# Windowed attention and a GEGLU block on one core: eight-token rows for the dilated heads, masks made on GpSimd, sums in banks of their own

## The chip, the core and the metric

The kernel runs on one core of a Trainium2 chip. A core has five engines with instruction streams of their own: TensorE (PE in the profile: matrix multiplies, with PEld for its weight loads), VectorE (DVE), ScalarE (ACT), GpSimd (POOL) and SyncE (SP, which here only issues DMAs). On-chip memory is SBUF, with 128 partitions; TensorE writes its results to PSUM, which has 8 banks of 512 fp32 columns per partition. DMA queues, fed by SP, ACT and POOL, bring data from HBM.

The metric is the time of one execution on the device, in microseconds. Three executions of the kernel before took 361.88, 362.62 and 362.64 us; the median is 362.62.

## What is computed

Attention with a causal window over 8 batches, 8 heads, 576 tokens and head size 64, then a gated FFN over the 4608 tokens. Heads 0 to 3 are plain: a query sees the last 32 keys. Heads 4 to 7 are dilated: it sees every fourth of the last 128 keys.

```python
scores = scale * np.matmul(q, k.transpose(0, 1, 3, 2))
rel = pos[:, None] - pos[None, :]
mask_plain = (rel >= 0) & (rel < window)                                       # window 32
mask_dil = (rel >= 0) & (rel < window * dilation) & (rel % dilation == 0)      # dilation 4
...
attn = attn / (np.sum(attn, axis=-1, keepdims=True) + 1e-09)
x = (attn @ v) reordered to (4608 tokens, 512)
...
gelu = 0.5 * g * (1.0 + erf(g * inv_sqrt2))      # g = x @ w_gate, d_ff = 1536
val = x @ w_val
return (gelu * val @ w_out)
```

Inputs and outputs are fp32; matmuls run on fp16 operands.

## The kernel before

**Unit of attention.** The work is cut into 32 pairs of heads, four to a batch: pair n belongs to batch n // 4, and its first two pairs are plain, the other two dilated. For a pair, `emit_s` writes scores (keys on partitions, queries on columns) into four PSUM banks and ACT takes the Exp into an fp16 tile `P`. Masking is done in one of two ways: TensorE first adds a bias (`bias_p` or `bias_d`, made from the masks) through the identity matrix, or DVE multiplies `P` by `mask_p` or `mask_d` (L379). `emit_pv` multiplies `P` with v (numerators, "num") and with a matrix of ones (the sums, "den"); both have 64 output partitions per head, so the two heads of a pair stand one above the other. With `wide` the sums have whole banks to themselves. `norm_r` transposes the sums (`dt`), takes reciprocals (`rc`) and spreads them (`rb`); `norm_x` multiplies numerators by `rb` into `xT`, the FFN's input with features on partitions.

**Dilated layout.** Token t belongs to class t mod 4, and a dilated head is a plain window of 32 within a class of 144 tokens. q and k of dilated heads are loaded with four tokens per row (`quads`): 128 rows of four tokens and a rest of 16 rows. `t_dil` transposes the 128 rows, `t_rest` the 16 rows. `kTr` holds the last keys of each class again (`last_keys`).

**The first two batches.** From batch 2 on, q and k are transposed by the DMA (`load_batch_rest`). For batches 0 and 1 TensorE does it with matmuls against the identity: plain heads from rows of six tokens (`sixes`, `t_plain`), dilated heads with `t_dil` and `t_rest`. Batch 0 stands ahead of everything. Its loads go out on SP and ACT: q and k of the plain heads, then of the dilated ones, then v. POOL issues loads of the identities and of the two masks, which the kernel carries as constants, then makes `bias_d`, casts the dilated q, issues the rest of v and the weights of block 0, casts v, and issues the other weights. DVE makes `bias_p`. TensorE runs 16 dummy matmuls (`warm`, L583) meanwhile. Then the four pairs of batch 0 follow in an order written out by hand, quoted below, in which the sums of pairs 0, 1, 2 and 3 go one after the other to the same banks (6 and 7), between other work.

```python
emit_s(0, 4, pe_mask=True); emit_s(1, 0, pe_mask=True)
...
den(0, 4, wide=True)
...                      # t_dil and t_rest of both dilated pairs, last_keys
den(1, 4, wide=True)
emit_s(2, 0, pe_mask=True)
num(0, 4)
den(2, 4, wide=True)
emit_s(3, 0, pe_mask=True)
num(1, 4)
den(3, 4, wide=True)
num(2, 0); num(3, 2)
```

**FFN stages.** The tokens come in 9 chunks (stages) of 512. A stage runs `ffn1` for 12 blocks (8 matmuls each: gate and value, L533; the first two blocks of stages 0 and 1 are interleaved in `ffn1_two`, L545), with Gelu on ACT (L557) and the GEGLU product on DVE (L558, `geglu`), then `ffn2` for four groups of 128 tokens (L564), and stores. Attention of later batches is woven in: `scores` and `values_b` name the pairs that stand in the `ffn2` part, `values_a` those between `ffn1` blocks of stages 3 to 6. Batch 1's transposes stand between the blocks 8 to 11 of stage 0.

**Plain pairs between ffn1 blocks.** Seven plain pairs of `values_a` go through `emit_both` (L455): v of a pair of heads is stored as v, ones, v (`vset`, three sets, the ones written once by DVE at L610 and L611), so that one matmul of full width gives numerators of a head on 64 partitions and its sums on the other 64. `norm_both_r` (L470) and `norm_both_x` (L480) then work on 64 partitions at a time, two instructions for a pair. `values_a` sets these pairs three or four blocks apart.

All instructions run in program order on each engine, across engines by semaphores; every tile of PSUM is one of the 8 banks, addressed by hand, so who waits for whom follows from the bank numbers.

Of the kernel before, what the change touches and what calls it, by code (L numbers as in the profile page):

```python
# [15 lines left out]
WIN = 32  # L16
DIL = 4
USCALE = 32.0


def _np_masks():
    p = np.arange(128)[:, None]

    def band(n, off=0):
        rel = np.arange(n)[None, :] + off - p
        return (rel >= 0) & (rel < WIN)

    main_p, last_p, tail_p = band(160), band(128), band(64, 64)
    main_d = band(128)

    rel = 48 + np.arange(16)[None, :] - p % 64
    rest_d = [(rel >= 0) & (rel < WIN) & (p // 64 == m) for m in range(2)]
    mp = np.concatenate([main_p, main_p, main_p, last_p, tail_p], axis=1).astype(np.float16)
    md = np.concatenate([main_d, rest_d[0], main_d, rest_d[1]], axis=1).astype(np.float16)
    return mp, md
# [3 lines left out]
def kernel(  # L39
# [19 lines left out]
    R6 = S // 6  # L59
    NCH = NT // CH  # L60
# [11 lines left out]
    mp_np, md_np = _np_masks()  # L72
    mp_dram = nc.inline_tensor(mp_np, name="mask_plain")
    md_dram = nc.inline_tensor(md_np, name="mask_dil")
    id_dram = nc.inline_tensor(np.eye(P, dtype=np.float16), name="attn_identity")
    id32_dram = nc.inline_tensor(np.eye(16, dtype=np.float32), name="identity_f32")

    const = ctx.enter_context(tc.tile_pool(name="const", bufs=1))
    psum = ctx.enter_context(tc.tile_pool(name="psum", bufs=1, space=bass.MemoryType.PSUM))
    ldp = ctx.enter_context(tc.tile_pool(name="ldp", bufs=1))  # L80
    qtp = ctx.enter_context(tc.tile_pool(name="qtp", bufs=2))
# [8 lines left out]
    ident32 = const.tile([16, 16], F32, tag="ident32")  # L90
# [9 lines left out]

    HP = HK // 2
    vset = [
        (
            const.tile([P, 4, HP, 3, D], F16, tag=f"vp{i}", name=f"vp{i}"),
            const.tile([P, HK, 4, D], F16, tag=f"vd{i}", name=f"vd{i}"),
            const.tile([P, HP, 3, D], F16, tag=f"vt{i}", name=f"vt{i}"),
            const.tile([P, HK, 2, D], F16, tag=f"vr{i}", name=f"vr{i}"),
        )
        for i in range(3)
    ]  # L110
# [11 lines left out]
    first_d = [x32[t][:, 0 : HK * 4 * D] for t in range(2)]  # L122
    first_r = [x32[2 + t][0:16, 0 : HK * 4 * D] for t in range(2)]
# [34 lines left out]

    def rows(src, b, kb):
        n = min(P, S - kb * P)  # L160
        return n, src[b, 0:HK, kb * P : kb * P + n, :].rearrange("h p d -> p h d")
# [8 lines left out]
    def new_v(b):  # L170

        sv = ldp.tile([P, 5, HK, D], F32, tag="sv", name=f"sv{b}")
        tiles["v", b] = vset[b % 3]
        return sv
# [6 lines left out]
    def v_cast(b, sv):  # L181
        vp, vd, vt, vr = tiles["v", b]
        nc.gpsimd.tensor_copy(
            vp.rearrange("p j g x d -> p (j g) x d")[:, :, 0:3:2, :],
            sv[:, 0:4].rearrange("p j (g x) d -> p (j g) x d", x=2),
        )
        nc.gpsimd.tensor_copy(vt[:, :, 0:3:2, :], sv[:, 4].rearrange("p (g x) d -> p g x d", x=2))
# [96 lines left out]
    def t_dil(b, hp, qd, q0, k0, engs):  # L284

        qtd_ = tiles["qT", b][1]
        for t, c0 in ((0, q0), (1, k0)):
            for hl in range(2):
                for m in range(2):
                    nc.tensor.transpose(  # L290
                        ps16f[:, c0 + (2 * hl + m) * P : c0 + (2 * hl + m + 1) * P],
                        qd[:, t, 2 * hp + hl, 2 * m : 2 * m + 2, :].rearrange("p r d -> p (r d)"),
                        ident,
                    )
        for t, c0 in ((0, q0), (1, k0)):
            copy(
                engs[t],
                qtd_[:, t, 2 * hp : 2 * hp + 2].rearrange("p h m i -> p (h m) i")[:, :, 0:P],
                ps16f[:, c0 : c0 + 512].rearrange("p (c i) -> p c i", i=P),
            )  # L300

    def t_rest(b, hp, rd, r0):

        qtd_ = tiles["qT", b][1]
        f32 = rd[0].dtype == F32
        pv = (psf if f32 else ps16f)[:, r0 : r0 + P]
        for t in range(2):
            for hl in range(2):
                for m in range(2):
                    c0 = (4 * t + 2 * hl + m) * 16  # L310
                    h0 = (2 * hp + hl) * 4 * D + 2 * m * D
                    nc.tensor.transpose(
                        pv[:, c0 : c0 + 16], rd[t][:, h0 : h0 + P], ident32 if f32 else ident[0:16, 0:16]
                    )
        nc.vector.tensor_copy(
            qtd_[:, :, 2 * hp : 2 * hp + 2].rearrange("p t h m i -> p t (h m) i")[:, :, :, P:NCL],
            pv.rearrange("p (t c i) -> p t c i", t=2, i=16),
        )
# [64 lines left out]
    def emit_pv(n, b0, parts=("num", "den"), wide=False):  # L383
# [17 lines left out]
        if is_plain(n):  # L401
            if "num" in parts:
                for j in range(5):
                    for hl in range(2):
                        lhs = vp[:, j, hp, 2 * hl, :] if j < 4 else vt[:, hp, 2 * hl, :]
# [38 lines left out]
    def emit_both(n, b0):  # L444


        b, hp = n // NHP, n % 2
        pt = tiles["P", n]
        vp, _, vt, _ = tiles["v", b]
        for hl in range(2):  # L450
            for j in range(5):
                w = (PW, PW, PW, P, PT)[j]
                p0 = j * PW - (32 if j == 4 else 0)
                trio = vp[:, j, hp] if j < 4 else vt[:, hp]
                nc.tensor.matmul(  # L455
                    ps[:, b0 + 2 * hl + j // 4, j % 4 * P : j % 4 * P + w],
                    trio[:, hl : hl + 2, :].rearrange("p x d -> p (x d)"),
                    pt[:, hl, p0 : p0 + w],
                    start=j in (0, 4),
                    stop=True,  # L460
                    skip_group_check=True,
                )

    def both_rows(half, b0, hl):
        return psf[64 * half : 64 * half + 64, (b0 + 2 * hl) * 512 : (b0 + 2 * hl) * 512 + S]

    def norm_both_r(n, b0):
        dt = nrm.tile([P, 18, 32], F32, tag="dt", bufs=1)
        for hl in range(2):
            nc.vector.transpose(  # L470
                dt[64 * hl : 64 * hl + 64].rearrange("p b c -> p (b c)"), both_rows(1 - hl, b0, hl)
            )
        recip(n, dt)

    def norm_both_x(n, b0):
        b, hp = divmod(n, NHP)
        rb = tiles.pop(("rb", n))
        for hl in range(2):
            half = slice(64 * hl, 64 * hl + 64)
            nc.vector.tensor_tensor(  # L480
                xT[hp][half, b * S : (b + 1) * S], both_rows(hl, b0, hl), rb[half], ALU.mult
            )

# [9 lines left out]
    def norm_r(n, b0, wide=False):  # L493
# [7 lines left out]
        recip(n, dt)  # L501

    def recip(n, dt):
# [84 lines left out]
    nc.gpsimd.dma_start(ident, id_dram.ap())  # L588
    nc.gpsimd.dma_start(mask_p, mp_dram.ap())
# [10 lines left out]
    qd0 = ldp.tile([P, 2, HK, 4, D], F16, tag="qd", name="qd0")  # L600
    new_qt(0)

    def r4(t):
        return fh(t).rearrange("p h (r d) -> p h r d", r=4)
# [231 lines left out]
```

The softmax here doesn't subtract the row's maximum and nothing guards it: scores larger than these inputs give would overflow.

## Time and profile before

| | |
|---|---|
| profiled execution, device time | 361.88 us |
| its span, first to last instruction | 359.8 us |
| mean granted TensorE clock | 0.985 |
| median of three executions | 362.62 us |
| FFN matmuls, L533 and L564, busy | 100.6 + 100.6 + 100.9 us |
| DVE busy, of it GEGLU products | 196.0 us, 72.6 us |
| POOL busy | 78.2 us |
| HBM read, written | 40.13 MB, 9.44 MB |

The profile is of one execution. A matmul of 512 columns is listed with about 380 ns, but they overlap: 96 of them take 20.72 us in the chain, 216 ns each. So a busy share of TensorE near 100% says that it has no gaps, not that it is at its peak. "Idle before" of an engine that isn't the bottleneck costs nothing. In a timeline, a line gives start, length, engine, line of the code, operation, output and inputs, and in brackets what ended the idle time before it.

### The profile page before, as it was taken

The page shows a single profiled execution, that of the slowest core. Times are in us where ns is not written, and L with a number is a line of the kernel's source. Part 1 is how long each engine was busy: PE and PEld are TensorE (multiplying, and loading weights), DVE is VectorE, ACT ScalarE, POOL GpSimd, SP SyncE. Part 2 cuts the span into 40 slices and gives each one's busy share as a digit, 9 for nine tenths or more (in the row PEclk, how much of TensorE's full clock was granted, in tenths as well). Part 3 has the DMA queues.
Part 4 walks back from the last instruction along what each step waited for, and adds up shares of the span by engine and source line. Part 5 has one row for each costly group of instructions (what it writes and reads, how often), then busy time and mean ns, then how long its engine had stood idle before and what let it go on. Part 6 is the DMA issues. An engine that isn't in the chain of part 4 may idle for free.

```text
span 359.8 us, 5997 instructions
## 1 busy us (share of the span) xinstructions
PE 344.5 (96%) x2358; PEld 166.2 (46%) x2358; DVE 196.0 (54%) x298; ACT 145.9 (41%) x212; POOL 78.2 (22%) x110
## 2 busy tenths in 40 slices
PE   6789999999989999899999999999999999999995
PEld 2554454444544445444444444544454444444442
DVE  3584446744266325765479838893679613403320
ACT  2633355244542345433653356436543123312321
POOL 2580434450531342063003410140000000000000
PEclk9959999999999999999999999999999999999999
DMA  8999999999999897599438952795100020011002
GB/s 208 232 183 215 209 159 195 199 141 239 192 119 228 178 157 144 139 168 153 94 106 186 148 97 88 178 168 68 60 29 0 21 97 2 1 66 52 0 29 87
DMA packets 107291, 45.30 MB, mean 126 GB/s; under 512 B 83040, under 2 KB 102496, under 8 KB 107264
## 3 DMA queue, kind: packets, MB, share of 16 engines
q1 hardware_dynamic: 84272, 31.21, 40.1%
q0 software_dynamic: 21456, 12.01, 25.8%
q10 hardware_dynamic: 1536, 1.70, 2.1%
q8 instruction: 18, 0.29, 0.3%
q14 instruction: 9, 0.07, 0.1%
HBM read 40.13 MB, written 9.44 MB: 138 GB/s over the span
## 4 chain that ended last, share of the span: by engine, by line
PE 88%; DVE 5%; DMA 3%; ACT 1%; issue 1%; ACTq 0%
PE ps L533 47%; PE ps L564 26%; PE ps L442 5%; PE ps L545 4%; DMA xT<-in_k_dram 3%; PE ps L369 2%; PE ps L339 1%; DVE dt L500 1%; DVE rb L507 1%; DVE xT L521 1%; PE ps L355 1%; PE ps L455 1%; PE ps L332 1%; ACT P L371 1%; DVE rc L505 0%
## 5 line engine op out<-in xcount | busy, mean ns | idle before, releaser
L558 DVE SCALAR_TENSOR_TENSOR u_all<-g,ps 128x512 f16<-128x512 f16 x108 | 72.6, 683 | 75.8 <-PE ps L533 65.7
L557 ACT ACTIVATE g<-ps 128x512 f16<-128x512 f32 x108 | 63.6, 597 | 123.6 <-PE ps L533 109.4
L564 PE MATMUL ps<-wo,u_all 128*128 128x512 f16 x432 | 100.9, 380 | 0.4 <-ACT osb L575 0.3
L533 PE MATMUL ps<-xT,wg 128*128 128x512 f16 x392 | 100.6, 379 | 0.2
L533 PE MATMUL ps<-xT,wv 128*128 128x512 f16 x392 | 100.6, 379 | 0.0
L564 PEld LDWEIGHTS <-u_all 128*128 128x128 f16 x432 | 39.2, 98 | 44.6 <-issue 0.5
L533 PEld LDWEIGHTS <-wv 128*128 128x128 f16 x392 | 38.3, 98 | 46.4 <-issue 0.2
L533 PEld LDWEIGHTS <-wg 128*128 128x128 f16 x392 | 37.3, 98 | 44.6 <-issue 2.1
L575 ACT ACTIVATE osb<-ps 128x512 f32<-128x512 f32 x33 | 19.7, 597 | 48.4 <-PE ps L564 48.4
L500 DVE STREAM_TRANSPOSE dt<-ps 128x576 f32<-128x576 f32 x25 | 19.5, 779 | 25.7 <-PE ps L442 25.6
L199 POOL CAST qp<-st 128x2048 f16<-128x2048 f32 x6 | 11.4, 1893 | 99.5 <-DMA st<-in_k_dram 61.3
L507 DVE STREAM_TRANSPOSE rb<-rc 128x576 f32<-128x576 f32 x32 | 24.9, 778 | 1.1
L371 ACT ACTIVATE P<-ps 128x1152 f16<-128x1152 f32 x16 | 18.1, 1129 | 13.1 <-PE ps L369 13.0
L349 ACT ACTIVATE P<-ps 128x960 f16<-128x960 f32 x16 | 15.5, 970 | 9.2 <-PE ps L339 9.1
L521 DVE TENSOR_TENSOR xT<-ps,rb 128x576 f16<-128x576 f32 x16 | 17.8, 1124 | 0.3
L545 PE MATMUL ps<-xT,wg 128*128 128x512 f16 x40 | 16.0, 400 | 1.4 <-DVE xT L521 0.9
L577 DVE TENSOR_SCALAR osb<-ps 128x512 f32<-128x512 f32 x3 | 2.1, 692 | 27.8 <-PE ps L564 27.8
L545 PE MATMUL ps<-xT,wv 128*128 128x512 f16 x40 | 15.9, 398 | 0.0
L442 PE MATMUL ps<-P,ones 128*64 128x192 f16 (+5 forms) x174 | 11.6, 248 | 2.0 <-ACT P L371 1.0
L379 DVE TENSOR_TENSOR P<-P,mask_p 128x1344 f16<-128x1344 f16 x10 | 9.1, 917 | 6.8 <-ACT P L350 6.8
L379 DVE TENSOR_TENSOR P<-P,mask_d 128x1152 f16<-128x1152 f16 x8 | 6.1, 757 | 11.1 <-ACT P L371 11.1
L470 DVE STREAM_TRANSPOSE dt<-ps 64x576 f32<-64x576 f32 x14 | 10.9, 781 | 0.4
(83 smaller groups left out, 268.4 us busy)
## 6 DMA issues: line engine op xcount, KB each, us to landing
out_dram<-osb SPq DMA_DIRECT2D x36, 256.0 KB, 2.0
sv<-in_v_dram SPq DMA_DIRECT2D x40, 128.0 KB, 3.5
st<-in_q_dram SPq DMA_DIRECT2D x24, 128.0 KB, 3.2
st<-in_k_dram SPq DMA_DIRECT2D x24, 128.0 KB, 2.9
qd<-in_q_dram POOLq DMA_DIRECT2D x7, 256.0 KB, 5.0
qd<-in_k_dram POOLq DMA_DIRECT2D x7, 256.0 KB, 6.7
vd<-in_v_dram POOLq DMA_DIRECT2D x7, 256.0 KB, 7.1
wg<-in_moe_w_gate_dram POOLq DMA_DIRECT2D x3, 512.0 KB, 7.7
```

Of the source, the lines that this page charges most:

```text
L349: nc.scalar.activation(pt[:, :, 0:PB], sb[:, 0, :, 0:PB], AF.Exp, bias=0.0, scale=scale)
L371: nc.scalar.activation(pt, ps[:, b0 : b0 + 4, 0:DW], AF.Exp, bias=0.0, scale=scale)
L442: nc.tensor.matmul(o, lhs, rhs, start=st, stop=True, skip_group_check=True)
L500: nc.vector.transpose(dst, den)
L507: nc.vector.transpose(rb.rearrange("p (b c) -> p b c", c=32), bass.AP(tensor=rc.tensor, offset=rc.offset, ap=[rc.ap[0], [1, 18], [0, 32]]),)
L521: nc.vector.tensor_tensor(dst.rearrange("p (i m s) -> p i m s", m=2, s=2), num, rb.rearrange("p (s m i) -> p i m s", s=2, m=2), ALU.mult,)
L533: nc.tensor.matmul(ps[:, b0 + gi, :], w[:, kc, ns], xT[kc][:, tok], start=(kc == 0), stop=(kc == NKC - 1))
L545: nc.tensor.matmul(ps[:, pairs[nb] + gi, :], w[:, kc, ns], xT[kc][:, tok], start=(kc == 0), stop=(kc == NKC - 1),)
L557: nc.scalar.activation(g, ps[:, b0, :], AF.Gelu)
L558: nc.vector.scalar_tensor_tensor(u_all[:, nb, :], g, USCALE, ps[:, b0 + 1, :], ALU.mult, ALU.mult)
L564: nc.tensor.matmul(ps[:, bank, :], u_all[:, fc, tb * P : (tb + 1) * P], wo_t[fc // 4][:, fc % 4, :], start=(fc == 0), stop=(fc == NNB - 1),)
L575: nc.scalar.activation(osb, ps[:, bank, :], AF.Copy, bias=0.0, scale=1.0 / USCALE)
```

## The change

- **Rows of eight tokens.** q and k of the dilated heads of batches 0 and 1 are loaded as 72 rows of eight tokens (`eights`), without a rest. `t_dil` makes 16 transposes of 72 columns for each pair (for q and k together) and two copies of 576 columns; `t_rest` and the fp32 identity are gone. For batch 0 the loads come in two halves of two heads; each half of q and k is cast by one instruction on 72 partitions (`cast_d`): two on DVE, one on POOL, one on ACT, the latter ahead of the first Exp.
- **Masks and identity** are made by POOL with memset and `affine_select`, in place of four loads; `bias_p` moves from DVE to POOL.
- **Batch 0 in another order.** Both dilated pairs are transposed right after the scores of the plain pairs, into banks 4 to 7. The sums of pair 0 go to banks 2 and 3, those of pair 1 to banks 0 and 1, those of pairs 2 and 3 to banks 6 and 7. The numerators of pairs 0 and 1 leave PSUM by an ACT copy, and POOL multiplies them (`num_split`). The weights of block 1 are issued ahead of POOL's casts of v, and those of block 2 after batch 0.
- **Plain pairs between ffn1 blocks** use `emit_pv(..., wide=True)`, `norm_r` and `norm_x` like the dilated ones: 10 matmuls for numerators and 6 for sums, of half width. The ones within v are gone, and v's tiles come from a pool of three. `values_a` sets pairs of stages 5 and 6 two blocks apart.
- `warm` has 20 matmuls instead of 16.

```diff
-    nc.gpsimd.dma_start(ident, id_dram.ap())
-    nc.gpsimd.dma_start(mask_p, mp_dram.ap())
...
+    nc.gpsimd.memset(ident, 1.0)
+    for sign in (1, -1):
+        nc.gpsimd.affine_select(
+            out=ident, in_=ident, pattern=[[sign, P]], compare_op=ALU.is_ge, fill=0.0, base=0, channel_multiplier=-sign
+        )
+    def band(t, step, off):
+        for sign, base in ((1, off), (-1, WIN - 1 - off)):
+            nc.gpsimd.affine_select(
...
+    nc.gpsimd.memset(mask_p, 1.0)
+    band(mask_p[:, 0:PB].rearrange("p (r c) -> p r c", c=PW), 0, 0)
+    band(mask_p[:, PB : PB + P].rearrange("p (r c) -> p r c", r=1), 0, 0)
+    band(mask_p[:, PB + P : PH].rearrange("p (r c) -> p r c", r=1), 0, 64)
+    nc.gpsimd.tensor_scalar(bias_p, mask_p, 1.0, 60000.0, ALU.subtract, ALU.mult)
+    nc.gpsimd.memset(mask_d, 1.0)
+    by_class = mask_d.rearrange("p (m i) -> p m i", m=2)
+    band(by_class[:, :, 0:P], 0, 0)
+    band(by_class[:, :, P:NCL], 64, 48)
+    nc.gpsimd.tensor_scalar(bias_d, mask_d, 1.0, 60000.0, ALU.subtract, ALU.mult)
...
+    def eights(src, b, h0, h1):
+        return src[b, h0:h1, :, :].rearrange("h (p r) d -> p h (r d)", r=8)
...
+        for t in range(2):
             for hl in range(2):
-                for m in range(2):
+                for r in range(4):
+                    c0 = ((hl * 2 + r % 2) * 2 + r // 2) * R8
                     nc.tensor.transpose(
...
+                        ps16[:, b0 + t, c0 : c0 + R8],
+                        q8[:, t, 2 * hp + hl, 2 * r : 2 * r + 2, :].rearrange("p r d -> p (r d)"),
+                        ident[0:R8, 0:R8],
...
-    warm(16, 7)
+    warm(20, 7)
...
+    cast_d("pool", 0, 0)
+    cast_d("dve", 1, 0)
+    cast_d("act", 1, 1)
+    cast_d("dve", 0, 1)
     load_v_dil_rest(0)
     load_w(0)
-    v_cast(0, sv0)
-    copy("pool", tiles["v", 0][1], r4(first_vd))
     w1 = load_w(1)
-    load_w(2)
...
+    def num_split(n, b0):
+        emit_pv(n, b0, ("num",))
+        rb = tiles.pop(("rb", n))
+        nc.scalar.copy(first_n[n], psf[:, b0 * 512 : b0 * 512 + S])
+        nc.gpsimd.tensor_tensor(xT[n][:, 0:S], first_n[n], rb, ALU.mult)
...
     emit_s(0, 4, pe_mask=True)
     emit_s(1, 0, pe_mask=True)
...
+    t_dil(0, 0, qd0, 4, ("dve", "dve"))
+    t_dil(0, 1, qd0, 6, ("act", "act"))
+    last_keys(0, 0, 2)
+    last_keys(0, 2, HK, nc.gpsimd)
+    v_cast(0, sv0)
+    copy("pool", tiles["v", 0][1], r4(first_vd))
+
+    den(0, 0, wide=True)
+    den(1, -2, wide=True)
+    emit_s(2, 4, pe_mask=True)
+    emit_s(3, 0, pe_mask=True)
+    den(2, 4, wide=True)
+    num_split(0, 4)
+    num_split(1, 4)
     den(3, 4, wide=True)
     num(2, 0)
     num(3, 2)
+    load_w(2)
...
-    values_a = {3: {4: 16}, 4: {2: 20, 6: 21}, 5: {1: 24, 4: 25, 7: 26}, 6: {1: 28, 4: 29, 7: 30, 10: 31}}
+    values_a = {3: {4: 16}, 4: {3: 20, 6: 21}, 5: {2: 24, 4: 25, 6: 26}, 6: {1: 28, 3: 29, 5: 30, 7: 31}}
...
-                (norm_both_x if is_plain(pend) else norm_x)(pend, SB)
+                norm_x(pend, SB)
...
-                if is_plain(pend):
-                    emit_both(pend, SB)
-                    norm_both_r(pend, SB)
-                else:
-                    emit_pv(pend, SB, wide=True)
-                    norm_r(pend, SB, wide=True)
+                emit_pv(pend, SB, wide=True)
+                norm_r(pend, SB, wide=True)
...
-                t_dil(1, hp, qd1, 4096 + 512 * hp, 5120 + 512 * hp, ("dve", "dve"))
-                t_rest(1, hp, (rr[:, 0], rr[:, 1]), 6144 + P * hp)
+                t_dil(1, nb // 11, qd1, 6 - 2 * (nb // 11), ("dve", "dve"))
```

## The prediction

> **What bounds the kernel now.** I read the page first: busy time by engine, then the chain that ended last.
>
> ```profile
> span 359.8 us, 5997 instructions
> PE 344.5 (96%) x2358; PEld 166.2 (46%) x2358; DVE 196.0 (54%) x298; ACT 145.9 (41%) x212; POOL 78.2 (22%) x110
> ...
> PEclk9959999999999999999999999999999999999999
> ...
> PE 88%; DVE 5%; DMA 3%; ACT 1%; issue 1%; ACTq 0%
> ```
>
> TensorE is the bound: its work for the FFN starts at about 26 us and hardly stops until the end. Two things can therefore move the time: when that stream starts, and how much TensorE work stands in it. One slice of the clock row is a 5: half clock. Next, the same chain in order of time, for the start (start, length, what):
>
> ```profile
> 1.19 12.33 DMA xT<-in_k_dram
> ...
> 14.07 0.78 DVE dt L500
> ...
> 16.84 0.67 PE ps L312 x8
> ...
> 19.34 1.14 ACT P L371
> ...
> 22.92 1.14 ACT P L371
> ...
> 24.10 1.73 PE ps L442 x24
> 25.83 4.88 PE ps L545 x16
> ```
>
> The start is a serial chain: loads until 13.5, transposes, the two dilated score groups one behind the other, numerators, and 16 FFN matmuls that take 4.88 us where 16 at full clock take 16 x 0.216 = 3.45 (the chain of 293.65 to 314.37 has 96 in 20.72). The first FFN pair ends at 30.7. Third, busy time by stretch (columns: TensorE, its weight loads, DVE, ACT, POOL, clock, DMA share, GB/s) shows why:
>
> ```profile
> 12.00:14.00 2.00, 0.88 (x18) 0.64 (x15) 0.46 (x1) 2.00 (x5) 0.75 (x2) 1.00 1.19 170
> 16.00:18.00 2.00, 1.16 (x15) 0.97 (x16) 1.21 (x5) 0.00 (x0) 1.42 (x2) 1.00 1.56 187
> 18.00:20.00 2.00, 2.00 (x26) 1.35 (x25) 1.91 (x4) 0.66 (x1) 1.92 (x3) 0.56 1.16 175
> 28.00:30.00 2.00, 2.00 (x10) 0.86 (x9) 0.77 (x1) 0.00 (x0) 0.76 (x1) 0.88 1.22 200
> ```
>
> TensorE is thinly used from 12 to 18, half clock is granted from about 18.2 and full clock again from about 28.5. Last, the timelines of POOL and TensorE for prices:
>
> ```profile
> 10.37 1.19 POOL L618 TENSOR_SCALAR bias_d<-mask_d 128x288 f16<-128x288 f16 x1 [6.82 <-DMA mask_d<-mask_dil]
> 18.08 1.04 POOL L183 CAST vp<-sv 128x1024 f16<-128x1024 f32 x1 [0.67 <-DMA sv<-in_v_dram]
> 19.06 0.41 POOL L187 CAST vt<-sv 128x256 f16<-128x256 f32 x1
> ...
> 64.26 0.43 PE L442 MATMUL ps<-P,vp 128*64 128x160 f16 x8
> ```
>
> [...] the drop at 18.2 follows a stretch made of transposes, and half clock lasts 10.2 us[...]. [...] the list of waits has TensorE's load for L442 waiting 0.4 us for DVE's dt, which reads the bank.
>
> **The change part by part.** *Plain pairs inside the FFN stages (7 of them).* Before, 10 full-width matmuls (L455) take 263.17 to 263.75 = 0.58. After, 10 numerators and 6 denominators at half width: 20 such matmuls stand in the chain at 0.66 to 0.71 each group; 10 numerators alone take 64.26 to 64.65 = 0.39, and six sums 59.88 to 60.29 = 0.41 with their drain. So 16 cost 0.66 to 0.80; I take 0.70: 7 x 0.12 = +0.84 (0.56 to 1.5). DVE saves a half-height transpose (0.78) and a multiply (0.75) each, 10.7 in all, but it waits for TensorE there (65.7 us idle before L558), so this is worth nothing. Pairs now stand two FFN blocks apart. After a pair's matmuls begin at P, DVE goes through dt, rc, rb, a GEGLU multiply and the last multiply; the dilated pair at 280.73 ended it at 285.12 = P+4.39, a plain one P+4.0. TensorE wants the bank at P+0.66+2x1.73 = P+4.12. Plain fits; dilated pair 30 ahead of 31 stalls 0.27 (0 to 0.5).
>
> *Dilated transposes of batch 1 in stage 0.* Before, 8+8 per pair occupy 42.64 to 43.49 and 49.71 to 50.54: 1.68 together. After, 16 of 72 columns; 12 of 96 take 45.23 to 45.74, 0.0425 each, so 0.68 per pair: -0.32 (0 to -0.5). DVE copies two 576-wide tiles (0.75 each, as L262 qTp) in place of 0.96 together; the next score group reads the second bank just then: +0.1 (0 to 0.3). Sum behind the start: 0.84+0.27-0.32+0.1 = +0.9 (0.2 to 2.0).
>
> *The start.* Removed: four POOL loads (273 KB of masks and identities). q and k of batch 0 stay 2.3 MB, in larger rows. At 341 GB/s, which the stretch around 9 us moves, the last dilated piece is usable about 0.8 before today's 13.5, at 12.7 (11.3 to 13.5); the first half about 10.5. The six memsets on DVE and 0.34 of bias_p leave DVE where it was idle: nothing.
>
> Added on POOL, ahead of its cast of q: three memsets (1088 columns), 12 selects (256+1344+576 = 2176 columns) and bias_p, bias_d. No row shows a select. Low: as casts, 0.83 ns per column and 0.19 each (from 1.04 and 0.41): 4.1 + 0.6 + 0.75 + 1.19 = 6.6. High: as TENSOR_SCALAR, 4.1 ns per column: 8.9+1.5+2.8+1.2 = 14.4. From 1.2 on, bias_d is done at 7.8 to 15.6[...]. I take 13.7; the cast (1.05) then ends at 14.8. Queued behind it on POOL: the two vr loads (1.33), then wg and wv of block 0, so wg is issued at 16.2 against 15.87. That load landed in time before (POOL's wait for wv ended at 25.69), so wv is there at about 26.1.
>
> On ACT the cast of k's second half now stands before the four exponentials. Those ran from 11.28; now cast 12.7 to 13.7, first pair's Exp to 15.1, second's to 16.3. The transposes of pair 2 write bank 4 and wait for that: 15.0, the same time as POOL's cast. TensorE has then had nothing from 12.3 to 15.0[...]. At half clock: 32 transposes of 72 columns (0.06 each) to 16.9; sums of pairs 0 and 1 to 18.1 (0.6 each); scores of pair 2, which need the ACT copies (two of 0.65 after 16.3, done 17.8), 18.1 to 19.7; Exp to 20.95. DVE: dt, rc, rb (1.93) of pair 0 from 17.7 and dt of pair 1 until 20.4, which frees the banks of pair 3: scores 20.4 to 22.0, Exp to 23.25. Then sums of pair 2 to 22.6, numerators 0 to 23.3, ACT copy to 24.0, numerators 1 to 24.7, copy to 25.5, sums of pair 3 to 25.3, numerators 2 and 3 to 26.4. POOL multiplies (576 columns, two inputs, about 1.5) end at 25.5 and 27.0; DVE multiplies at 28.4 and 29.5. FFN: 26.45, half clock until 28.48[...]; then full clock: pair ends at 30.9 to 31.0. The chain of before has 30.7 for the same point, so +0.3. What was saved (no repeated waits between sums and scores) is paid back by the late Exp and the half clock.
>
> **Sum.** +0.3 and +0.9 give +1.2. The profiled execution took 361.88, of which 359.8 is the span; the median of the three runs, 362.62, lies 0.74 above it, and the shift carries over: 363.8.
>
> **Rivals.** *A: the start gets faster* (the other side). If selects cost like casts and nothing is loaded, POOL is out of the way at 8.9, transposes begin right behind the first Exp at about 14, and if loads come at 11.3, at 13. At full clock the same walk gives FFN from 24.2 and the pair's end at 28.3 to 29: -2.0, with +0.9: 361.5 and down to 360.7. It decides once POOL's cast ends before about 13.5 and the drop of the clock stays at 18.2 or later. For it: the serial chain quoted has four separate waits that separate banks remove. Against it: Exp behind a load.
>
> *B: POOL is late.* [...] every later step, and the weights behind it, moves by 3.5: 367. For it: 1.19 us for 288 columns. Against: one sample.
>
> *C: full clock returns a window later*, at 31.9: 16 matmuls from 26.45 at 0.427 leave 3.2 at that point, the end at 32.6, +1.9 and 0.9: 365.4. For it: TensorE was busy some 6 of the 6.8 us from 18.2 to 25.1, and that did not bring it back.
>
> *D: parts cancel:* the start gains 0.9, 362.6. That the change doesn't do what it says I leave out: the order of instructions shows the new queues.
>
> **Chances.** Likeliest 0.38 (363.3 to 364.4), A 0.24, B 0.12, C 0.14, D 0.12. A measurement here tells 0.2%, 0.7 us, from none. Faster: A, and a little of D, 0.25. Same: the rest of D and the low edge of the likeliest, 0.18. Slower: 0.57. The range leaves out half of B and the far half of A: 361.0 to 366.4.
>
> **What would show it.** Right: POOL's cast of q ends near 15, ACT's first Exp starts after a cast that waited for a load, half clock begins near 15, the first FFN pair ends near 31, and 16 matmuls per plain pair take 0.70. Wrong: the pair ends under 30 (A), POOL still building masks at 14 (B), or clock back after 30 (C).

## The result and the profile after

Four executions of the changed kernel took 363.90 to 364.54 us, with a median of 364.33; the kernel before had 362.44. The ratio is 1.0053, with a 95% interval of 1.0036 to 1.0070: slower by half a per cent, 1.9 us (1.3 to 2.5). The profiled execution took 364.49 us, of which 362.8 is the span, 3.0 more than the span of the profiled execution before. First, lines of the page after that answer to those shown of before:

```profile
span 362.8 us, 6082 instructions
PE 347.0 (96%) x2404; PEld 165.6 (46%) x2404; DVE 185.4 (51%) x272; ACT 147.6 (41%) x214; POOL 85.6 (24%) x122
...
PEclk9958999999999999999999999999999999999999
...
PE 87%; DMA 5%; DVE 5%; ACT 2%; issue 1%; ACTq 0%; SPq 0%; DVEq 0%
```

TensorE is still the bound, now with 2.5 us more of busy time. DVE has 10.6 us less, and nothing came of it. The half-clock slices of the clock row are a 5 and an 8 now, where there was one 5. Next, the chain of waits after, in order of time (start, length, what), for the start:

```profile
2.05 12.59 DMA xT<-in_k_dram
...
14.66 0.03 ACT qd L262
...
15.62 0.97 ACT P L335
...
16.63 1.98 PE ps L295 x32
18.60 0.72 PE ps L428 x5
...
22.04 1.12 PE ps L341 x4
...
27.95 4.83 PE ps L488 x16
```

The second half of k lands at 14.64. ScalarE's cast of it ends at about 15.7, only then does the first Exp start, and TensorE's transposes wait for that Exp until 16.63. The interleaved FFN pair (L488) begins at 27.88. I count it as ended when the first matmul of the next block starts: 32.62, where it was 30.55 before (the prediction's 30.7 is the end of the last matmul in the chain). The same stretches as before (columns: TensorE, its weight loads, DVE, ACT, POOL, clock, DMA share, GB/s):

```profile
12.00:14.00 2.00, 0.65 (x12) 0.42 (x11) 0.89 (x1) 0.00 (x0) 2.00 (x4) 1.00 0.92 197
...
18.00:20.00 2.00, 2.00 (x24) 1.23 (x22) 1.47 (x3) 1.34 (x3) 0.60 (x2) 0.50 1.25 210
28.00:30.00 2.00, 2.00 (x6) 0.62 (x6) 1.97 (x4) 0.41 (x1) 2.00 (x3) 0.50 0.08 14
30.00:32.00 2.00, 2.00 (x10) 0.90 (x9) 0.89 (x1) 0.00 (x0) 2.00 (x4) 0.88 0.87 189
```

Half clock runs from 16.8 to 30.5, 13.7 us, where it was 18.2 to 28.5 before, 10.2 us. In all profiles here such stretches are multiples of 3.41 us, so I speak of windows: four instead of three. Their number isn't fixed by the kernel, as the table of experiments shows. From 28 to 30 almost nothing is loaded (14 GB/s): GpSimd issues block 2's weights only at 28.53, behind its two multiplies of the start. Timelines of GpSimd, before:

```profile
21.85 0.77 POOL L127 DMA_DIRECT2D wg<-in_moe_w_gate_dram  x1
...
23.31 0.79 POOL L207 DMA_DIRECT2D qd<-in_q_dram  x1
```

and after:

```profile
25.69 2.89 POOL L583 TENSOR_TENSOR xT<-xT,rb 128x576 f16<-128x576 f32 x2 [3.58 <-ACT xT L582]
28.53 0.80 POOL L126 DMA_DIRECT2D wg<-in_moe_w_gate_dram  x1
...
30.06 0.77 POOL L615 DMA_DIRECT2D qd<-in_q_dram  x1
```

Behind the start I divide at the point where stage 1 of the FFN begins. From 32.62 to there it takes 36.74 us, against 37.56 before: 0.82 less. From there to the end of the span it takes 293.4, against 291.7: 1.7 lost. So 2.07 - 0.82 + 1.7 = 2.95, the 3.0 of the spans. The medians differ by only 1.9; the other 1.1 lies in which executions were profiled. Where the 1.7 are, the chain shows in stage 6. Before:

```profile
259.88 3.45 PE ps L533 x16
263.33 0.59 PE ps L455 x10
263.92 5.18 PE ps L533 x24
269.10 0.59 PE ps L455 x10
269.68 5.18 PE ps L533 x24
```

and after:

```profile
262.16 3.45 PE ps L476 x16
265.62 0.70 PE ps L428 x16
266.32 3.56 PE ps L476 x16
269.88 0.70 PE ps L428 x16
```

A plain pair takes 0.70 instead of 0.59, as forecast. But the 16 FFN matmuls behind it take 3.56 instead of 3.45 as well. Before, 24 of them behind a full-width pair took 5.18 (0.216 each), and behind a dilated pair, which is half-width, 5.29. So the full-width matmuls behind half-width ones take about 0.11 more in all, and a plain pair costs 0.22, twice the forecast. (Ends of matmuls are modelled, so the sum of a pair and the block behind it, 4.26 against 4.04, is firmer than its two parts.)

### The profile page after: what moved, and what is told of

Its sections match the earlier page's. It is cut to its first block, busy times and chain, and to the rows that moved or that the text cites. A ratio compares the mean times of both kernels' runs of the same rounds, so it can differ in the third digit from the quotient of the medians.

```text
span 362.8 us, 6082 instructions
## 1 busy us (share of the span) xinstructions
PE 347.0 (96%) x2404; PEld 165.6 (46%) x2404; DVE 185.4 (51%) x272; ACT 147.6 (41%) x214; POOL 85.6 (24%) x122
## 4 chain that ended last, share of the span: by engine, by line
PE 87%; DMA 5%; DVE 5%; ACT 2%; issue 1%; ACTq 0%; SPq 0%; DVEq 0%
PE ps L476 46%; PE ps L507 25%; PE ps L428 6%; PE ps L488 4%; DMA xT<-in_k_dram 3%; DMA out_dram<-osb 2%; PE ps L355 1%; PE ps L325 1%; DVE xT L464 1%; PE ps L341 1%; DVE dt L446 1%; DVE rb L450 1%; PE ps L295 1%; PE ps L318 1%; DVE u_all L501 1%
## 5 line engine op out<-in xcount | busy, mean ns | idle before, releaser
L501 DVE SCALAR_TENSOR_TENSOR u_all<-g,ps 128x512 f16<-128x512 f16 x108 | 73.6, 687 | 85.1 <-PE ps L476 75.4
L446 DVE STREAM_TRANSPOSE dt<-ps 128x576 f32<-128x576 f32 x32 | 25.0, 780 | 27.0 <-PE ps L428 26.3
L488 PE MATMUL ps<-xT,wg 128*128 128x512 f16 x40 | 16.0, 399 | 1.4 <-DVE xT L464 0.9
L520 DVE TENSOR_SCALAR osb<-ps 128x512 f32<-128x512 f32 x3 | 2.1, 690 | 28.8 <-PE ps L507 28.8
L488 PE MATMUL ps<-xT,wv 128*128 128x512 f16 x40 | 15.9, 398 | 0.0
L428 PE MATMUL ps<-P,ones 128*64 128x96 f16 (+5 forms) x216 | 15.2, 258 | 0.0
L190 POOL CAST vp<-sv 128x1024 f16<-128x1024 f32 x8 | 8.7, 1090 | 11.9 <-DMA sv<-in_v_dram 11.9
## 6 DMA issues: line engine op xcount, KB each, us to landing
wo<-in_moe_w_out_dram POOLq DMA_DIRECT2D x3, 512.0 KB, 10.2
```

Of the source, the lines that this page charges most:

```text
L428: nc.tensor.matmul(o, lhs, rhs, start=st, stop=True, skip_group_check=True)
L446: nc.vector.transpose(dst, den)
L488: nc.tensor.matmul(ps[:, pairs[nb] + gi, :], w[:, kc, ns], xT[kc][:, tok], start=(kc == 0), stop=(kc == NKC - 1),)
L501: nc.vector.scalar_tensor_tensor(u_all[:, nb, :], g, USCALE, ps[:, b0 + 1, :], ALU.mult, ALU.mult)
```

## The experiments

All ratios are to the kernel before on the same chip (median 362.06 to 362.36 there), so ratios compare across chips better than medians do. The start of an execution shifts with the clock's windows, so beside each ratio I give four marks of one profiled execution: how long half clock was granted in the start, when the first FFN pair ends, when stage 1 starts, and the time from there to the end of the span.

| kernel | median us | ratio to before (95%) | half clock | pair ends | stage 1 starts | to the end |
|---|---|---|---|---|---|---|
| before | 362.44 | 1 | 10.2 | 30.55 | 68.1 | 291.7 |
| after | 364.33 | 1.0053 (1.0036 to 1.0070) | 13.7 | 32.62 | 69.4 | 293.4 |
| e1_late | 364.33 | 1.0053 (1.0032 to 1.0074) | 3.4 | 28.82 | 68.4 | 293.5 |
| e2_fill | 363.57 | 1.0040 (1.0023 to 1.0056) | 0 | 30.07 | 68.4 | 293.4 |
| e3_both | 363.17 | 1.0037 (1.0022 to 1.0052) | 3.4 | 29.99 | 68.7 | 291.7 |
| e4_wide | 363.71 | 1.0043 (1.0027 to 1.0059) | 13.7 | 31.90 | 68.8 | 293.1 |
| e5_masks | 366.79 | 1.0123 (1.0099 to 1.0148) | 13.7 | 33.20 | 71.5 | 293.4 |
| e6_quads | 365.51 | 1.0088 (1.0068 to 1.0108) | 13.7 | 33.43 | 70.2 | 293.2 |
| e7_wo | 362.26 | 1.0007 (0.9989 to 1.0025) | 6.8 | 29.32 | 66.1 | 293.4 |
| e7b_place | 362.86 | 1.0009 (0.9993 to 1.0025) | 10.2 | 29.68 | 66.7 | 293.4 |
| e8_best | 361.78 | 0.9994 (0.9978 to 1.0011) | 10.2 | 29.84 | 67.7 | 291.8 |
| e10_beforewo | 362.27 | 0.9998 (0.9983 to 1.0013) | 13.7 | 31.70 | 68.5 | 291.7 |
| e11_wo | 364.77 | 1.0079 (1.0049 to 1.0109) | 6.8 + 3.4 | 31.28 | 69.5 | 293.4 |
| e12_masks | 362.31 | 1.0009 (0.9998 to 1.0021) | 13.7 | 33.01 | 69.9 | 291.8 |

My first theory: the start is late because of ScalarE's cast and the clock, and the gate stages cost what their half-width products cost. The rivals: GpSimd's masks hold the start, or the start doesn't matter.

The column of half clock has to be read first. e3_both, described below, has the start of the changed kernel: its first Exp begins at 15.48 (15.62 in the changed kernel's profile) and TensorE waits 3.89 (3.97) before the transposes. Yet its pair ends 2.6 earlier, at 29.99. What differs between the two starts is the clock: half clock was granted for one window instead of four. The same stretches of both (columns as above, over 5 us each), changed kernel:

```profile
20.00:25.00 5.00, 4.43 (x46) 2.82 (x45) 3.48 (x7) 2.29 (x3) 2.11 (x3) 0.50 1.24 207
25.00:30.00 5.00, 4.34 (x44) 2.84 (x44) 4.29 (x8) 2.53 (x3) 4.22 (x4) 0.50 0.73 121
```

and e3_both:

```profile
20.00:25.00 5.00, 3.38 (x63) 2.43 (x62) 4.38 (x8) 2.90 (x4) 2.48 (x4) 0.91 1.24 207
25.00:30.00 5.00, 4.45 (x43) 2.18 (x40) 3.87 (x5) 2.27 (x3) 5.00 (x6) 1.00 0.94 130
```

So the end of the pair is compared below only between profiles with equally long half clock, or with its length beside it.

**e1_late: ScalarE's cast behind the Exps.**

```diff
-    cast_d("act", 1, 1)
     cast_d("dve", 0, 1)
...
     emit_s(1, 0, pe_mask=True)
+    cast_d("act", 1, 1)
```

> The changed kernel (364.3 us) with one move: ACT's cast of k's second half stands behind the four Exp instructions of the plain pairs instead of ahead of them. Theory 1 (the start is late because the Exps stand behind a cast that waits for a load): the first Exp starts at about 11.3 instead of 15.6, TensorE's dilated transposes at about 13 instead of 16.6, and the first FFN pair ends 1.0 to 1.5 us earlier, 363.0 us. Rival (the late load itself, or the half clock, sets the start, whatever ACT does first): the first Exp moves but the pair's end doesn't by more than 0.4 us, 364.0 us.

The first FFN pair ends 3.8 us earlier than in the changed kernel, and the median time is the same. About 2.6 of the 3.8 is the clock: against e3_both, with the same 3.4 us of half clock, the cast's place is worth 1.2, and between kernels with 10.2 us in all (e7b_place and e8_best, which have this edit, against e11_wo) 1.4 to 1.6. That is near the 1.0 to 1.5 that I expected of the start; the expected gain in time didn't come. The chain of waits of e1_late tells why:

```profile
16.78 12.82 DMA wv<-in_moe_w_val_dram
...
30.04 12.31 DMA st<-in_k_dram
...
42.40 2.36 POOL qp L264 x3
44.76 0.70 POOL wo L132
45.46 7.45 DMA wo<-in_moe_w_out_dram
```

It runs through loads for 36 us: block 1's values, behind them batch 1's plain q and k, GpSimd's casts of these, and behind the casts on GpSimd's queue the issues of wo's second and last third (the load shown is the last). TensorE's timeline of e1_late shows the waits that this makes (in brackets, the idle time before a line and what ended it):

```profile
42.90 0.43 PE L295 MATMUL ps<-ident,qd 72*128 72x72 f16 x8 [1.55 <-DMA qd<-in_k_dram]
...
52.95 1.89 PE L507 MATMUL ps<-wo,u_all 128*128 128x512 f16 x8 [0.22 <-DMA wo<-in_moe_w_out_dram]
...
60.21 0.48 PE L428 MATMUL ps<-P,ones 128*64 128x512 f16 x6 [0.79 <-DVE P L365]
```

The start's gain became waits for batch 1's dilated k, for wo, and at 60.21 for a DVE multiply. e2_fill and e3_both end the pair at about 30 and start stage 1 at 68.4 and 68.7, with waits for the same loads.

**e2_fill: 14 dummy matmuls between the scores of pairs 0 and 1, to hold the clock.**

```diff
     emit_s(0, 4, pe_mask=True)
+    warm(14, 0)
     emit_s(1, 0, pe_mask=True)
```

> The changed kernel with 14 dummy matmuls of 512 columns (3.0 us) between the scores of pairs 0 and 1, where TensorE otherwise waits from 12.7 to 16.6. They compute nothing that is used. Theory 2 (half clock from 16.8 to 30.5 is a large part of the late start): full clock holds longer, the first FFN pair ends 1.5 to 2.5 us earlier, 362.3 us. Rival (the start is bound by loads, ACT and DVE, and the clock costs only what the FFN pair shows): full clock at most shifts, and the pair ends within 0.5 us of 32.6; if the dummies delay the scores of pair 1, it gets later. 364.3 us.

The clock stayed full from 5.8 on (0.999 on average over the span) and the pair ended 2.6 earlier; stage 1 started 1.0 earlier. The rest went into the same chain of loads. What the dummies gain isn't shown: e3_both's pair ends as early without them, and the ratio's interval overlaps the changed kernel's.

**e3_both and e4_wide: the gate's part undone, and the gate's part alone.** e3_both is the changed kernel with v as v, ones, v and `emit_both` again, at the places of before. e4_wide is the kernel before with this alone:

```diff
-                (norm_both_x if is_plain(pend) else norm_x)(pend, SB)
+                norm_x(pend, SB)
...
-                if is_plain(pend):
-                    emit_both(pend, SB)
-                    norm_both_r(pend, SB)
-                else:
-                    emit_pv(pend, SB, wide=True)
-                    norm_r(pend, SB, wide=True)
+                emit_pv(pend, SB, wide=True)
+                norm_r(pend, SB, wide=True)
```

> The changed kernel with the seven plain pairs between ffn1 blocks as they were before (one matmul for numerators and sums, and their old places); all else as changed. Theory 3 (these stages cost 1.7 us: 0.23 for each pair and one stall of a dilated pair): 362.6 us, and from the start of stage 2 to the start of stage 7 the chain takes as long as in the kernel before. Rival (the later stages cost what I forecast, 1.1 us, and the rest is drift between executions): 363.2 us.

> The kernel before (362.4 us) with the half-width numerators and sums for the seven plain pairs, at the places of before, three or four blocks apart. Theory 3 (0.23 us for each pair; the stall comes only from the closer places): 362.4 + 1.6 = 364.0 us, with no wait of TensorE for DVE in stage 6. Rival (most of the loss is the closer spacing): under 363.0 us.

From stage 1 to the end e3_both takes the 291.7 of before and e4_wide 293.1: seven pairs at 0.2 are 1.4, and the other 0.3 belong to the new places (0.16 of it is the wait ahead of pair 31, below). So the gate's cost is shown from both sides. The time of e3_both missed my 362.6, though: by the ratios e4_wide costs 1.6 us, and 1.3 are left in e3_both, in its start and stage 0; together more than the 1.9 measured, within the intervals.

**e5_masks: masks and identity loaded again, into the changed kernel.**

```diff
-    nc.gpsimd.memset(ident, 1.0)
...
+    nc.gpsimd.dma_start(ident, id_dram.ap())
+    nc.gpsimd.dma_start(mask_p, mp_dram.ap())
+    nc.gpsimd.dma_start(mask_d, md_dram.ap())
...
+    nc.vector.tensor_scalar(bias_p, mask_p, 1.0, 60000.0, ALU.subtract, ALU.mult)
```

> The changed kernel with masks and identity as constants that GpSimd loads behind the first loads (273 KB more to read), the plain pairs' bias again one VectorE operation, the dilated pairs' bias still GpSimd's. Theory (GpSimd's building of them isn't on the path: in the changed kernel its cast of q at 11.30 waits for the load, not for the masks): the first pair of FFN blocks ends between 32.3 and 33.3 (32.6 with the masks built on the chip, or up to 0.7 later if the 273 KB push back k's second half), ratio to the kernel before 1.004 to 1.008. Rival (GpSimd's work at the start costs the time): the first pair ends below 31.5 and the ratio falls to 1.002 or less.

The first pair ends within my range, but by the ratios the time is 2.5 us above the changed kernel's, and the ratio is outside of it. k's second half landed at 15.7, 1.0 later, and GpSimd waited 9.07 us for `mask_d`, so its cast of q began at 13.78 instead of 11.30. Every load that GpSimd issues came later with it, and batch 1's transposes then waited (chain of e5_masks):

```profile
28.30 0.68 POOL xT L579
...
31.20 0.73 POOL qd L611
31.92 14.80 DMA qd<-in_k_dram
...
46.77 0.43 PE ps L286 x8
```

In the changed kernel, making the masks on GpSimd thus gains over loading them on its queue.

**e6_quads: batch 0's dilated q and k in rows of four again (128 rows and a rest of 16), in halves.**

```diff
-                in_=eights(src, 0, HK + 2 * g, HK + 2 * g + 2),
+                in_=quads(src, 0, HK, 0, 4 * P)[:, 2 * g : 2 * g + 2],
...
-    t_dil(0, 0, qd0, 4, ("dve", "dve"))
+    t_dil0(0, 4, ("dve", "dve"))
```

> The changed kernel with batch 0's dilated q and k again in rows of four tokens (128 partitions and a rest of 16), still in two halves per tensor, with casts and transposes to match (32 instead of 64 of them, of 128 columns or 16). Theory (the loads to 72 partitions move slower, which makes k's second half land at 14.6 instead of the 12.7 that I forecast, and that starts the chain through the ScalarE cast, the Exp and the transposes): k's second half lands at 13.0 to 13.8, the transposes start about 1 us earlier, the first pair of FFN blocks ends at 31.0 to 32.0, and the ratio to before is 1.003 to 1.005. Rival (the landing is set by the bytes alone, or by another queue): k's second half lands at 14.3 or later and the first pair ends at 32.3 to 33.3.

The landing moved as the theory said: k's second half came at 13.5 instead of 14.6. The pair ended later all the same. The transposes began at 15.04, 1.6 earlier, but with the rests there are 64 matmuls between 128-row and 16-row weights, and they held TensorE until 20.0, where the 32 of the changed kernel end at 18.5. In this kernel ScalarE's table load (1.28) also stood behind its first wait, at 8.74 instead of 3.27, which moved its first cast by 1.5. So the run shows the landing, not a clean price of rows of eight.

**e7_wo and e7b_place: e1_late, and wo's second third issued ahead of the casts; e7b_place sets batch 1's transposes a block later as well.**

```diff
     load_wo(0)
+    wo1 = load_wo(1)
     q61 = ldp.tile([R6, 2, 6, HK, D], F16, tag="qp", name="qp1")
...
-    wo1 = load_wo(1)
     wo2 = load_wo(2)
```

> As e1_late, and GpSimd issues the load of wo's second third ahead of the four casts of batch 1's plain q and k (at about 30 instead of 44.8). Theory (in e1_late the start's gain of 3.8 us is lost in the load stream of stage 0 as a whole: there the transposes of batch 1's dilated pair waited 1.55 for qd at 42.9, and ffn2 0.22 for wo): wo no longer ends a wait, but it takes its bytes from qd and st of batch 1, so that these waits grow; stage 1 starts at 67.8 to 69.0 (e1_late 68.5), ratio 1.003 to 1.007. Rival (the issue of wo behind the casts is the bound): stage 1 starts below 67.5, ratio below 1.003.

> As e7_wo, and the transposes of batch 1's pairs stand one FFN block later (plain at blocks 10 and 11, dilated at 9 and 11, instead of 9, 10 and 8, 11). Theory (load stream): the later place hides about 1.7 us of the wait for qd and st, stage 1 starts at 66.5 to 67.8 and the ratio is 0.999 to 1.003. Rival (what holds stage 1 back is not these loads but the PE work, or later loads of v and wo): stage 1 starts at 68.3 or later, ratio 1.004 or more.

For e7_wo the rival was right. Stage 1 starts at 66.1, 3.3 earlier than in the changed kernel, and the ratio falls by 0.0046, with intervals that don't overlap. Between the first FFN pair and stage 1 only one wait is left on TensorE, 0.26 for a DVE copy, which the changed kernel has too (timeline of e7_wo):

```profile
50.48 0.26 PE L325 MATMUL ps<-qTp 64*128 64x128 f16 x4 [0.26 <-DVE qTd L266]
```

From the pair's end to stage 1 it takes 36.75, the 36.74 of the changed kernel: this is TensorE's own work there, and what other rows of the table have above it (39.62 in e1_late) is waits. Of those in e1_late some 1.0 go with the edit. wo has landed in time, which is 0.22. SP issues batch 1's plain v only once wo's second third has landed (`gate`), so GpSimd's cast of v moved from 58.41 to 54.76. In e1_late it stands beside DVE's mask multiply, of which the chain has 1.54 from 58.63; here the chain has none of that multiply, and the wait of 0.79 for it is gone. The wait of 1.55 for batch 1's dilated k is gone for another reason: in this execution GpSimd came out of the start's multiplies 1.3 earlier than in e1_late, and k landed at 41.31 instead of 42.85. So the ratios show the gain of 1.7, and the profile shows some 1.0 of it. e7b_place falls into its theory's range, but the later place brought nothing beyond e7_wo.

**e11_wo: the early wo alone, in the changed kernel.** The edit is that of e7_wo.

> The changed kernel with that edit alone (wo's second third issued ahead of the casts), its slow start left as it is. Theory (with the first pair ending at 32.6 PE is the bound of stage 0 and the loads have time): stage 1 starts at 69.0 to 69.7, ratio 1.004 to 1.0065, as without the edit; the gain of e7_wo needs both edits. Rival (the early wo alone gains): stage 1 starts below 68.5, ratio below 1.003.

No gain: stage 1 starts where it did, and the ratio is a little worse than I expected. TensorE now waits for batch 1's dilated q and k, beside whose loads wo's is under way (timeline of e11_wo):

```profile
43.76 0.43 PE L295 MATMUL ps<-ident,qd 72*128 72x72 f16 x8 [0.23 <-DMA qd<-in_q_dram]
45.10 0.43 PE L295 MATMUL ps<-ident,qd 72*128 72x72 f16 x8 [0.91 <-DMA qd<-in_k_dram]
```

So each edit alone is worth nothing, and both together 1.7 us.

**e10_beforewo: the same edit in the kernel before.**

> The kernel before with one edit: wo's second third issued ahead of the four casts of batch 1's plain q and k. Theory (before's first pair of FFN blocks ends at 30.55, and no wait of its stage 0 was for wo; only the loads of v and batch 2 behind it move up): stage 1 starts at 67.3 to 68.3 (68.1 before), the 0.62 stall at 59.9 can go, ratio 0.997 to 1.001. Rival (wo and what is gated on it is a bound in before too): stage 1 starts below 67.0, ratio below 0.997.

As expected, no difference in time; stage 1 starts at 68.5, past my 68.3, since this execution's start was 1.15 later. The wait of 0.62 at 59.88 that the profile of before has is gone, and stage 0 takes 36.83 from the pair's end instead of 37.56. That isn't the edit's doing: e4_wide, whose start and stage 0 are those of before, has no such wait either and takes 36.85.

**e12_masks: the kernel before with the masks made by GpSimd alone.** The edit is the mask part of the change's diff.

> The kernel before with the mask part of the change alone: masks and identity built by GpSimd, plain bias by GpSimd; its identity in fp32 is still loaded. Theory (273 KB less ahead of k and no GpSimd wait for the mask's load, as e5_masks shows from the other side, where the loads cost 1.0 at k's landing and 2.2 at stage 1's start): dilated k lands 0.5 to 1.1 earlier than the 13.5 of before, the first pair ends at 29.4 to 30.2, stage 1 starts at 67.0 to 68.0, ratio 0.995 to 0.9995. Rival (GpSimd's 14 us at the start hold its cast of q back, or the gain meets the load of wo): stage 1 starts at 68.0 or later, ratio 0.9995 to 1.003.

This one missed, by a flaw of the edit. The identity in fp32, which `t_rest` needs, is still loaded, and its issue now stands behind the masks on GpSimd's queue (chain of e12_masks):

```profile
9.76 1.18 POOL bias_d L154
...
11.00 6.02 DMA ident<-identity_f
...
17.06 0.83 PE ps L343 x8
```

k landed at 13.25, only 0.3 earlier, and TensorE waited 1.99 for that identity; still the time is that of before. What the masks alone would gain in the kernel before stays open.

**e8_best: e3_both, e1_late and e7_wo together.**

> The changed kernel with three edits together: ScalarE's cast behind the Exps (e1_late), wo's second third issued ahead of the casts (e7_wo), and the plain pairs of the gate stages as before the change (full-width products for numerators and sums together, e3_both). Theory (the three effects add: start -3.8 us, kept by the early wo as in e7_wo, and gate stages -1.8 us): stage 1 starts at 65.8 to 66.8, from there to the end 291.3 to 292.0, ratio to before 0.994 to 0.998, faster than both kernels. Rival (the gate's 1.8 us and the start's gain meet in another load, that of batch 2 or 3): stage 1 starts at 67.5 or later, ratio 0.999 or more.

The rival's marks came: it is 2.1 us faster than the changed kernel by the ratios, but not shown to be faster than before, since the interval takes in 1. All but one of its times lie between 358.65 and 364.03, a wider range than that of any other kernel here. In the profiled execution the gate stages were those of before (291.8), but batch 0's v landed only at 18.4, the multiplies of the start on GpSimd ended at 26.2, and behind them came the issue of batch 1's dilated q:

```profile
24.81 1.39 POOL xT L635
...
27.68 15.19 DMA qd<-in_q_dram
...
42.92 0.82 PE ps L302 x16
```

TensorE waited 0.83 there. The gains add only in part; what this profile shows of it is that GpSimd's queue couples the start to the loads of stage 0.

## Why the prediction was right, and where it wasn't

**The time and the sign** were right: 363.8 forecast, 364.33 measured, slower. The forecast difference was +1.2, the measured one +1.9. In the profiled executions the parts behind the start came to +1.7 - 0.82 = +0.88, beside the +0.9 forecast; that agreement is luck, as the terms show:

| term, us | forecast | measured |
|---|---|---|
| seven plain pairs in the gate stages | +0.84 | +1.54 |
| wait ahead of pair 31 | +0.27 | +0.16 |
| batch 1's transposes | -0.32 | -0.64 |
| score group behind their copies | +0.1 | +0.44 |
| start | +0.3 | +2.07 in the profiles; +0.7 to +0.9 at equally long half clock (an estimate) |
| sum | +1.2 | 2.2 to 2.4 with that estimate; the medians have 1.9 (1.3 to 2.5) |

**Plain pairs in the gate stages.** "I take 0.70: 7 x 0.12 = +0.84" held for the pair itself: 0.70 against 0.59. This is the term that was sized too small: missing was the way back, 0.11 for the first full-width matmuls after each pair, 7 x 0.11 = 0.77. The row for it was in the profile of before, 5.29 against 5.18 for 24 matmuls. 0.77 + 0.77 + 0.16 is the 1.7. That DVE's saving would be worth nothing held.

**Batch 1's transposes.** 16 of 72 columns take 0.52 a pair (0.0325 each), not 0.68, and 1.68 - 1.04 gives -0.64. The score group behind the DVE copies takes 0.84 instead of 0.40, of which 0.26 is the wait for them. Together -0.20, where -0.22 was forecast: two errors that cancel. The other 0.62 of the 0.82 is a wait of TensorE for DVE in the profile of before (timeline of before):

```profile
59.88 0.48 PE L442 MATMUL ps<-P,ones 128*64 128x512 f16 x6 [0.62 <-DVE P L379]
```

It is not the change that removes it: e4_wide has before's stage 0 without this wait, and the changed kernel's stage 0 has it in e1_late (0.79) and e3_both (0.81). In the profile of before that multiply takes 1.51 from 58.31 (0.86 from 54.22, where GpSimd is idle), and GpSimd's cast of `vt` beside it takes 1.03 from 59.05. In the changed kernel's profile the same cast stands alone, at 58.18, with 0.40, and the multiply behind it, at 60.26, takes 0.82. The multiply isn't always longer beside the cast: in e7b_place the cast took 1.03 as well (from 57.61), and the chain has 0.83 of the multiply from 57.56.

**The start.** The first steps held: ScalarE's cast waits for k, Exp stands behind it, and TensorE idles 3.97. The terms that failed: "usable ... at 12.7" was 14.64, since the loads in 72 rows moved slower than the rate I took (e6_quads, with 128 rows, has 13.5); and full clock came back at 30.48 instead of 28.48 (the time in the profile of before), which is rival C's event; C's return at 31.9 is 28.48 and one window of the 3.41 us that the profiles show. No trace of before showed that half clock would begin near 15; it began at 16.83. But most of the +2.07 is not the change. The kernel before's start had 10.2 us of half clock in its own profile and 13.7 in e4_wide and e10_beforewo; the changed kernel's had 13.7, in e3_both 3.4 and in e11_wo 10.2 in two parts. At 13.7 the pair ends at 31.9 and 31.7 with the start of before and at 32.62 with the other; at 10.2 at 30.55 and 31.28. So the start costs 0.7 to 0.9, an estimate from these five profiles. That the change's idle time makes the clock drop isn't shown: it dropped at 16.3 to 18.2 with the start of before as well, where no such gap stands. In the 3.41 us ahead of the drop TensorE was busy for 2.46 in the kernel before, 1.79 of them transposes, and for 0.20 in the changed one.

In the changed kernel's profile TensorE was busy for 3.41 us in the window from 16.83, 1.77 of them transposes, for 2.92 in the one from 20.24 and for 2.68 in the one from 23.66; full clock came only after the next, with 3.41 and no transposes. In e3_both it came back after the first window, at 20.9 (a clock of 0.91 from 20 to 25). What brings it back isn't shown beyond that; the last section has other profiles.

GpSimd was earlier than I had it: `bias_d` ended at 10.96, not 13.7 (the two prices gave 7.8 to 15.6), and its cast of q then waited for the load. GpSimd's timeline of the changed kernel:

```profile
1.09 0.65 POOL L95 TENSOR_SCALAR_AFFINE_SELECT ident<-ident 128x128 f16<-128x128 f16 x2
...
2.41 2.38 POOL L102 TENSOR_SCALAR_AFFINE_SELECT mask_p<-mask_p 128x480 f16<-128x480 f16 x6
...
9.78 1.18 POOL L122 TENSOR_SCALAR bias_d<-mask_d 128x288 f16<-128x288 f16 x1
11.30 1.03 POOL L264 CAST qd<-xT 72x1024 f16<-72x1024 f32 x1 [0.35 <-DMA xT<-in_q_dram]
```

With that rival B falls, whose 3.5 us no trace showed: the kernel's first memset on GpSimd starts at 0.81, and from there to 10.96 GpSimd is busy for 9.28 of 10.15 us. One sum of mine was off without weight: three memsets at the prices of casts are 1.5, not 0.6 (they took 1.2).

**The step that failed most** is one that didn't show in the time: I carried each shift of the first FFN pair one to one to the end. e1_late reached the start of rival A (28.8; I had 28.3 to 29), in good part by the clock, and its median is 364.33, not 361.5. Between the start and stage 1 stand loads that GpSimd issues. The change moved block 2's weights and batch 1's dilated q and k behind the multiplies of the start, from 21.85 and 23.31 to 28.53 and 30.06, and my walk through the start left this move out. In the changed kernel's profile the late start hides these loads: TensorE waits for none of them. With an earlier one they are the next bound (e1_late, e2_fill, e3_both), and e7_wo shows that the order on GpSimd's queue is worth 1.7 us then.

## What to carry to other kernels

Before pricing an earlier start, follow the loads of the next stage and the queue that issues them: a start is worth only what those loads allow, and two edits can each be worth nothing alone and 1.7 us together. Price narrow matmuls by the stretch behind them too, not by their own row (here half of the 0.22 us). Where the granted clock changes in windows, compare marks of several profiles, and only those with equally long half clock, before putting a difference of 1 us or more down to an edit: here 2.6 us of the start came and went with the windows alone.

## What the runs showed of the hardware

- Full-width matmuls behind half-width ones took about 0.11 us more in all: 3.56 against 3.45 for 16 matmuls in the changed kernel, 5.29 against 5.18 for 24 in the kernel before. Behind score groups, whose matmuls read 64 partitions, 16 take the same 3.56 (kernel before, at 209.00).
- In 13 of the 14 profiles half clock was granted in the start, in whole windows of 3.41 us. In the kernel before TensorE was busy for 2.89, 2.90 and 3.41 us in its three, in the changed kernel for 3.41 (1.77 of them transposes), 2.92, 2.68 and 3.41 in its four; full clock came back after the last of each. In eight more profiles (e5_masks to e12_masks, from rows of 1 us) the windows before full clock came back have 3.3 to 3.4 us busy, the others at most 3.0, but for the first of e6_quads: 3.4, with transposes until 20.0, the first 3.0 us of it.
- The time of one and the same kernel went with the granted clock. Of 33 executions of the kernel before on one chip, 11 had a mean clock of at most 0.982 and a mean span of 360.7; 9 had at least 0.990 and 359.5. The correlation of the two is -0.76; on two other chips it is -0.62 (35 executions) and -0.41 (52).
- GpSimd's 12 selects over 2176 columns took 4.9 us, about 2.2 ns a column; a two-step tensor-scalar over 672 columns took 2.48, which is 3.7 ns a column. Selects cost neither as casts nor as tensor-scalars, the two ends that I had taken.
